# A fused attention and gated feed-forward kernel: another way in for the first quad's keys and queries, and a new order

## The chip, the cores and the metric

The kernel runs on one core of one Trainium2 chip. The metric is the device time of one execution in microseconds (us), the median of three runs.

The core has five engines that matter here: TensorE (PE, with PEld for its weight loads), VectorE (DVE), ScalarE (ACT), GpSimd (POOL) and SyncE (SP). Each engine takes its instructions in the order in which the program issues them, and waits on semaphores for what other engines and DMAs produce. DMAs are issued by POOL, SP and ACT, each into a queue of its own; all of them share 16 DMA engines. In this kernel only DMAs that POOL issues change the type of the data on the way (fp32 in DRAM, bf16 in SBUF).

## The reference

```python
# q, k, v: (8, 12, 448, 64) fp32; w_gate, w_val: (768, 1536); w_out: (1536, 768)
scores = (1 / sqrt(64)) * q @ k.T
attn   = max(scores, 0) ** 2 / 448
y      = attn @ v                              # (8, 12, 448, 64)
x      = y.transpose(0, 2, 1, 3).reshape(3584, 768)
out    = (max(x @ w_gate, 0) * (x @ w_val)) @ w_out
```

It is attention with a squared ReLU in the place of the softmax, then a feed-forward block with a ReLU gate. All inputs and the output are fp32.

## The kernel before, in words

**Tiling.** Four heads of one batch make a *quad*; there are 8 batches of 3 quads. A sequence of 448 is split into 7 blocks of 64. For each quad the keys lie in partitions 64 to 127 of a `raw` tile and the queries in partitions 0 to 63, in bf16. The `raw` tiles of the first two batches lie in `gvT`, a tile that is needed for other things only later (`early_raw`), so the trace names them `gvT`. Keys and queries must be transposed, so that the head dimension lies in partitions: the first six quads on PE against an identity matrix (L503 and L510 for batch 0, L550 for batch 1), with copies out of PSUM into `qkT` on DVE or ACT (L478, L476); the other 18 quads by a permuting copy on DVE into the one buffer `perm` (L574) and two DMA transposes that SP issues (L580).

**Attention.** A score step S is a group of four 64x64-tiled matmuls into two PSUM banks for each key block (L648), then a ReLU out of PSUM on ACT or DVE (L659, L661) and a square on ACT or DVE (L671, L673). Then come the products with the values, PV (L690), and a copy into `xT` (L706 on ACT, L708 on DVE). In batch 0 the queries are split: the first three blocks (192 columns, `QT` = 3) are loaded, transposed and used first, the other four later (`q_late`, transposed at L510).

**Feed-forward.** Batches 0 and 1 use plain products with `wg` and `wv` (L755, ReLU on ACT at L763, product on DVE at L765). The other batches use Strassen's scheme in pairs (L864), with sums of the weights made by DVE; the output products are L979, in the same scheme, and the results go out through SP's queue (L951).

**What sets the order.** Nothing is scheduled at run time: `plan` (L228) simulates the machine with a list of costs and emits the instructions in order of their planned start. PE's order is given by hand-over letters, `PE_ORDER`: a lower-case letter takes the next but so many of the list of attention operations, an upper-case letter the same of the feed-forward list. `LOAD_ORDER` does the same for POOL's list of loads. All other operations (`others`: copies, ReLUs, squares, stores, DMA transposes) are placed by the planner when they can start; `AHEAD` gives each a wait, in tenths of a microsecond around the letter m, that moves it against its rivals. `Res` holds, for each buffer, the planned time from which it is free; `Buf.pick` takes the buffer that is free first. In `commit`, a buffer's release is written down when its last reader is planned, from that reader's planned end; the planned end of a DMA can still move afterwards, as `flow` shares the DMA engines between loads and transposes. While PE would idle in the first 32 us, `plan` puts in matmuls on constants, which `filler` makes (L1133, on a tile that a memset at L1120 fills).

**The first loads.** `load_qk` (L429) makes for each quad a load of the keys, all seven blocks, and in batch 0 a load of the first three query blocks, all by `dma_in` on POOL (L388, the helper's line for all of them). With the letters before, POOL issues in this order: keys and queries of quad 0, keys and queries of quad 1, queries of quad 2, keys of quad 2, then late queries and values. `transpose_first` makes for quad 0 two PE operations: T0 for the first three blocks, of keys and queries together (12 transposes), and T0k for the other key blocks (16 transposes); T0k also waits for `key_ops`, which is empty before. `PE_ORDER` begins with T0, T0k and score steps of quad 0. The transposes of quads 1 and 2 (at L503 too) come further on. The identity matrix is made by DVE, until 3.15 us in the trace.

Of the kernel before, what the change touches and what calls it, by code (L numbers as in the profile page):

```python
# [8 lines left out]
FP32 = mybir.dt.float32  # L9
# [6 lines left out]
class Res:  # L16


    def __init__(self, n):
        self.free = {i: 0.0 for i in range(n)}  # L20


class Buf:
# [7 lines left out]
    def pick(self, now=0.0):  # L31

        best = None
        for i in self.among:
            if all(i + w in self.res.free for w in range(self.width)):
                t = max(self.res.free[i + w] for w in range(self.width))
                if best is None or max(t, now) < max(best[0], now):
                    best = (t, i)
        return best


class Op:


    def __init__(self, engs, emit, deps=(), alloc=(), reads=(), mode=None, grp=None):
        self.engs, self.emit = engs, emit
        self.deps, self.alloc, self.reads = list(deps), list(alloc), list(reads)
        self.mode, self.grp = mode, grp
        self.load = self.land = self.share = 0.0
        self.kind = self.behind = None  # L50
        self.xbar = 0
        self.start = self.end = self.eng = None
        for b in self.reads:
            b.readers += 1


class Planner:
# [5 lines left out]
    TO_LOAD, LOADED = 2.35, 0.95  # L63
    TO_TURN, TURNED, TURN = 1.7, 0.8, 3.65
    ISSUE = 0.28
    FILL_FROM = 0.4
    FILL_COLD = 5.5
    FILL_UNTIL = 32.0
# [13 lines left out]
    QT = 3  # L82
# [6 lines left out]

    def __init__(self, banks):  # L90
        self.banks = banks
        self.t = {"POOL": 1.25, "DVE": 0.85, "ACT": 2.0}
        self.ops = []
        self.mode = None
        self.dma_t = 0.0
        self.queues = [], []
        self.loads = []
# [21 lines left out]
    def best(self, op):  # L119
        r = self.ready(op)  # L120
        if r is None:
            return None
        c = None
        for e, (occ, busy) in op.engs.items():
            if e in ("DVE", "ACT"):
                r = max([r] + [d.end + self.MARGIN for d in op.deps if d.load])
            s = max(r, self.t.get(e, 0.0))
            if e == "PE" and op.mode != self.mode:
                s = max(r, self.t.get(e, 0.0) + self.SWITCH)
            f = s + busy + (self.BIAS if e == "DVE" and len(op.engs) > 1 else 0.0)  # L130
            if c is None or f < c[0]:
                c = (f, s, e)
        return c[1], c[2], r
# [27 lines left out]
    def commit(self, op, s, e):  # L161
        assert op.behind is None or op.behind.start is not None
        op.start, op.eng = s, e
        occ, busy = op.engs[e]
        now = self.now(op)
        self.t[e] = s + occ
        op.end = s + busy
        if e == "PE":
            self.mode = op.mode
        if op.load:  # L170
            self.loads.append(op)
            self.transfer(0, op, s + self.TO_LOAD, op.load)
        elif op.xbar:
            self.transfer(1, op, s + self.TO_TURN, self.TURN)
        else:
            op.end += op.land
        for b in op.alloc:
            t, b.idx = b.pick(now)
            assert t <= s + 1e-6
            for w in range(b.width):  # L180
                del b.res.free[b.idx + w]
            b.last = op.end
        for b in op.reads:
            b.readers -= 1
# [8 lines left out]
PE_ORDER = (  # L193
    'aaceccaacbcbacaeibbeccabaaecabAAacaFAccACaaabgcbaaNKJKATAHaaaJCICcebeJEEIbbFbaaGADFafabBABEabaBBAAabfeAKTLabKK'
    'CCGbaCDCAhecddHBBbbaDGACafbdaDDbaaFCAAbgbdAAacACBbaAAhcbbCaabABBbaDAAAebbaCcaaBIABCBcBABEEBAADCBAGAAHAEBBCBAAB'
    'DfaAADaaCABAcBBABaaACBAacbabDAAFCAACBCFCHBAEBCcBAAACbaAACAGAabbBABaaBCADAecbEACAaAFebaBACEAabEEFABfaFgaaABbdiA'
    'caCeaGBABBecdCAcbaAAAABfabaAEKADBAQAAEAAACBAAAbaDBAbbBDABAdaGCAAaabAAECAaBABBAAbaAIBAAbbaDAAbcAAJBCBAHAAFacBFA'
    'CbaACBACAAgbaAECEACBAedCAAbaaAFCAAAAAeaaaICcaAAbaAABAaaaaBBcbaCJEACaBEJAKAADBAACABAAABCBBBACBCDCBAABAAAADADHCB'
    'DCBICHABCFBHACAFEBEHBABCAEGBBDBBDCCECAAAGBABBABBBCGEAABBCBCCBABBABBBA'
)  # L200
# [4 lines left out]
AHEAD = (  # L205
    'mlmmmolklollknkknkmplknmkjnnnmolnlmmnqlkmoqokonmjkmkmokimmkloohjrnlghglokjjklmmqngmhtlhprneoficpkmjjsfnnpwrtpg'
    'arogqkpqrainsvngkgjgjzorsopgfnlrljmjoprmpskjjdbhgmmttnkmrlwpellhjpnjkqpqrlnlqlskbktfsijmkppnnjgkqllpmfhrkrlloh'
    'qtorjsllojjfkgpprlrhkmnppqlqoljlpmlnnrlooorlohholmjnlpofrwqmnfloogmisphjnnnhijlkqilojnokqkiomoorllqohglslmmmhn'
    'smlowookpgijmqkqmpjjrflkinkjiimhqpqommkljnnonompjslgpppjhornftieqplmirwlkthrihsurmosnrjfnmgvnhjnsrqoslhomntmol'
    'mvliqeknljmkmqsqlhmpsilnjklimmapnrqlnmdjgokqqnnorpigtjqitsoomkggjihpntqtqnenkpkiiuoposrepoqlnthjmkplplkkkkmsio'  # L210
    'irqvpnimlemgqspnnnbtukjkinnqjhgkkmqcisldokjnmqknkmklklofqnlpfnknqhlmknomgljilsiknjsnijlipknjmmpkjnrjlmqepmnflh'
    'ghknornoimjpoljkpmoqjiorpofnlplnnkrbmqpgompihkkkisqinkijffhlqpurmqpovfmgmgnnoorlompkoljpnnlqomlkopskhoihmkmnok'
    'onoiooemgipikpjimfknjomqmoipontjlkopgooljjlpmrjkifmhohpdjloliqokpmrligmhsufqrtosfrhrggpronqqkkmjmmlsqqlqtqoooq'
    'gmqikmklrspkmjrmonpihjponiinpmhmogphpmpnjqmklkoonlipgilmkmjnkjingpnqkmojsnklmkjrqmpmklhgknllfrlgqkjknmlfjnrrmp'
    'slmrmnnnikmonninkjmmmqjlikpqqmnjohpijopklkn'
)


# [74 lines left out]
def kernel(  # L293
# [10 lines left out]
    nc = tc.nc  # L304
# [3 lines left out]
    B, H, S, D = q.shape  # L308
# [5 lines left out]
    NT = S // P2  # L314
# [10 lines left out]
    QT = Planner.QT  # L325
# [29 lines left out]
    hT = pool.tile([128, KF, 2 * S], BF16, name="hT")  # L355
# [28 lines left out]
    others, pool_ops = [], []  # L384


    def dma_in(dst, src, n_desc, us, deps=(), alloc=(), share=0.25):
        op = Op({"POOL": (0.5 + 0.0004 * n_desc,) * 2}, lambda: nc.gpsimd.dma_start(out=dst(), in_=src),  # L388
                deps=deps, alloc=alloc)
        op.load, op.share = us, share  # L390
        pool_ops.append(op)
        return op
# [31 lines left out]
        o = 2 * NQ * 4 * NT * D + (NQ * b + g - 3) * n  # L424
        return flat[:, o:o + n].rearrange("p (h t d) -> p h t d", h=2, t=NT)

    FIRST_K = {(0, 0): 0.75, (0, 1): 2.4, (0, 2): 1.25}

    def load_qk(b, g):  # L429
        st = quads[(b, g)] = Quad()  # L430
        hs = slice(4 * g, 4 * g + 4)
        early = b < NEARLY
        st.raw_buf = None if early else Buf(r_raw)
        st.raw = lambda: early_raw(b, g) if early else raw_t[st.raw_buf.idx]
        src = lambda x, t0=0, t1=NT: x[b, hs].rearrange("h (p t) d -> p h t d", t=NT)[:, :, t0:t1]
        st.key_ops = []
        if (b, g) == (0, 0) and Planner.SPLIT:
            st.load_k = lambda t0, t1: dma_in(lambda: st.raw()[64:128, :, t0:t1], src(k, t0, t1), 256, 0.16 * (t1 - t0))
            k_op = st.load_k(0, QT)
        else:  # L440
            k_op = dma_in(lambda: st.raw()[64:128], src(k), 256, FIRST_K.get((b, g), 1.1),
                          alloc=[] if early else [st.raw_buf])
        if b == 0:
            st.load_q = lambda t0, t1: dma_in(lambda: st.raw()[0:64, :, t0:t1], src(q, t0, t1), 256, 0.17 * (t1 - t0))
            q_op = st.load_q(0, QT)
        else:
            q_op = dma_in(lambda: st.raw()[0:64], src(q), 256, 1.1)
            q_op.behind = None if early else k_op
        st.qk_ops = [k_op, q_op]
        if (b, g) == (0, 0) and Planner.SPLIT:  # L450
            st.key_ops = [st.load_k(QT, NT)]

    def load_v(b, g):
        st = quads[(b, g)]
# [669 lines left out]
    def filler(us, cold):  # L1124

        pb = bank([7, 6, 5, 4, 3, 2, 1, 0])
        total = int(us * (1200 if cold else 2400))
        n = (total + S - 1) // S
        width = max(64, total // n)

        def emit():
            for _ in range(n):
                nc.tensor.matmul(ps[:, pb.idx, :width], lhsT=still[:, :128], rhs=still[:, :width], start=True, stop=True)  # L1133

        return Op({"PE": (us, us)}, emit, deps=[still_op], alloc=[pb], reads=[pb])

    for g in range(NQ):
        load_qk(0, g)
# [106 lines left out]
```

## Time and profile before

| what | value |
|---|---|
| median of three runs | 404.07 us (403.68 to 406.75) |
| the profiled execution's own time | 403.12 us |
| its span in the trace | 401.3 us, granted TensorE clock 0.999 |
| PE busy | 391.8 us (98%), of it 8.4 us filler matmuls at L1133 |
| DVE busy | 323.7 us (81%) |
| ACT busy | 273.6 us (68%) |
| POOL busy | 75.6 us (19%), issuing DMAs |
| POOL's DMA queue | 23.60 MB written, 43.4% of 16 engines' span |
| SP's and ACT's queue | 18.89 MB |
| read from HBM | 47.19 MB |

The span is the stretch from the first to the last instruction that the profiler recorded; the execution's time has 1.8 us around it. A line of the timeline gives start, length, engine, line of the kernel, operation, output<-input, how many instructions are merged, and in brackets the idle time of the engine just before it and what ended that. A line of the table by stage gives the busy time of the engines in a stretch, with the number of instructions. PE counts as busy with filler matmuls too, so their time has to be taken off. All tiles of a kind have one name: `gvT` covers the early `raw` tiles, `ps` all PSUM banks.

### The profile page before, as it was taken

The page shows a single profiled execution, that of the slowest core. Times are in us where ns is not written, and L with a number is a line of the kernel's source. Part 1 is how long each engine was busy: PE and PEld are TensorE (multiplying, and loading weights), DVE is VectorE, ACT ScalarE, POOL GpSimd, SP SyncE. Part 2 cuts the span into 40 slices and gives each one's busy share as a digit, 9 for nine tenths or more (in the row PEclk, how much of TensorE's full clock was granted, in tenths as well). Part 3 has the DMA queues.
Part 4 walks back from the last instruction along what each step waited for, and adds up shares of the span by engine and source line. Part 5 has one row for each costly group of instructions (what it writes and reads, how often), then busy time and mean ns, then how long its engine had stood idle before and what let it go on. Part 6 is the DMA issues. An engine that isn't in the chain of part 4 may idle for free.

```text
span 401.3 us, 8739 instructions
## 1 busy us (share of the span) xinstructions
PE 391.8 (98%) x3471; PEld 208.7 (52%) x3471; DVE 323.7 (81%) x563; ACT 273.6 (68%) x402; POOL 75.6 (19%) x121
## 2 busy tenths in 40 slices
PE   8899999999999999999999999999999999999995
PEld 4576655454555554544445554444455555555563
DVE  4896777999899869989989978889878857758662
ACT  4897777788898547959878767778678854333221
POOL 8954541013212200213100121400100000000000
PEclk9999999999999999999999999999999999999999
DMA  8999999995996972386968697770503320000255
GB/s 116 191 200 200 199 183 191 175 113 77 166 127 138 195 140 36 41 115 80 111 113 147 145 160 107 101 118 9 73 23 80 80 59 2 0 0 2 59 125 133
DMA packets 77305, 43.44 MB, mean 108 GB/s; under 512 B 40912, under 2 KB 77264, under 8 KB 77264
## 3 DMA queue, kind: packets, MB, share of 16 engines
q0 software_dynamic: 34896, 23.60, 43.4%
q1 hardware_dynamic: 42048, 18.89, 26.0%
q8 instruction: 27, 0.44, 0.4%
q10 hardware_dynamic: 320, 0.39, 0.3%
q14 instruction: 14, 0.11, 0.1%
HBM read 47.19 MB, written 11.01 MB: 145 GB/s over the span
## 4 chain that ended last, share of the span: by engine, by line
PE 74%; DMA 16%; issue 6%; POOL 2%; DVE 1%; SPq 0%; DVEq 0%; POOLq 0%
PE ps L864 36%; PE ps L979 18%; PE ps L755 8%; PE ps L648 6%; PE ps L690 5%; DMA qkT<-perm 5%; DMA wg<-in_moe_w_gate_dram 5%; DMA vv<-in_v_dram 3%; DMA gvT<-in_v_dram 2%; DMA gvT<-in_k_dram 1%; POOL vv L388 1%; DVE perm L574 0%; POOL gvT L388 0%; POOL raw L388 0%; DVE at L661 0%
## 5 line engine op out<-in xcount | busy, mean ns | idle before, releaser
L659 ACT ACTIVATE at<-ps 128x896 bf16<-128x896 f32 (+3 forms) x119 | 105.5, 911 | 21.2 <-PE ps L648 20.6
L811 ACT COPY f<-ps 128x448 f32<-128x448 f32 x101 | 53.1, 533 | 46.8 <-PE ps L864 31.7
L671 ACT ACTIVATE at<-at 128x896 bf16<-128x896 bf16 (+2 forms) x72 | 66.8, 938 | 2.3 <-DVE at L661 1.2
L673 DVE TENSOR_TENSOR at<-at 128x896 bf16<-128x896 bf16 (+3 forms) x99 | 59.0, 612 | 5.5 <-ACT at L659 4.5
L661 DVE TENSOR_SCALAR at<-ps 128x896 bf16<-128x896 f32 (+4 forms) x52 | 54.5, 1050 | 6.3 <-PE ps L648 6.0
L388 POOL DMA_DIRECT2D vv<-in_v_dram x44 | 26.6, 610 | 136.3 <-PE ps L648 133.9
L648 PE MATMUL ps<-qkT 64*64 64x448 bf16 (+2 forms) x756 | 50.3, 338 | 2.0 <-ACT at L659 0.9
L864 PE MATMUL ps<-sx,wv 128*128 128x448 bf16 x216 | 50.8, 353 | 0.0
L864 PE MATMUL ps<-xT,gvT 128*128 128x448 bf16 x216 | 50.2, 353 | 0.0
L864 PE MATMUL ps<-xT,wg 128*128 128x448 bf16 x216 | 50.1, 353 | 0.0
L864 PEld LDWEIGHTS <-gvT 128*128 128x128 bf16 x324 | 31.0, 98 | 30.6 <-issue 2.7
L979 PEld LDWEIGHTS <-sh 128*128 128x128 bf16 x312 | 29.2, 98 | 23.9 <-issue 4.7
L979 PEld LDWEIGHTS <-hT 128*128 128x128 bf16 x270 | 25.6, 98 | 19.9 <-issue 3.4
L979 PE MATMUL ps<-wo,hT 128*128 128x384 bf16 x192 | 35.4, 326 | 0.0
L690 PE MATMUL ps<-at,vv 64*64 64x448 bf16 (+2 forms) x700 | 33.9, 328 | 0.2 <-DMA vv<-in_v_dram 0.2
L648 PEld LDWEIGHTS <-qkT 64*64 64x64 bf16 x756 | 18.9, 105 | 27.7 <-issue 23.8
L969 DVE SCALAR_TENSOR_TENSOR o<-ps,f 128x384 f32<-128x384 f32 x41 | 22.5, 554 | 12.6 <-PE ps L979 7.9
L813 ACT ACTIVATE f<-ps 128x384 f32<-128x384 f32 x38 | 18.6, 492 | 20.3 <-PE ps L979 20.0
L755 PE MATMUL ps<-xT,wv 128*128 128x448 bf16 (+2 forms) x180 | 31.0, 316 | 0.3 <-DVE hT L765 0.3
L864 PEld LDWEIGHTS <-wv 128*128 128x128 bf16 x216 | 20.3, 98 | 20.8 <-issue 3.0
L864 PEld LDWEIGHTS <-wg 128*128 128x128 bf16 x216 | 20.6, 98 | 20.1 <-issue 1.8
L755 PE MATMUL ps<-xT,wg 128*128 128x448 bf16 (+2 forms) x180 | 30.9, 315 | 0.1
(71 smaller groups left out, 488.8 us busy)
## 6 DMA issues: line engine op xcount, KB each, us to landing
out_dram<-o SPq DMA_DIRECT2D x108, 96.0 KB, 2.2
vv<-in_v_dram POOLq DMA_DIRECT2D x44, 112.0 KB, 5.3
raw<-in_k_dram POOLq DMA_DIRECT2D x18, 224.0 KB, 5.0
raw<-in_q_dram POOLq DMA_DIRECT2D x18, 224.0 KB, 7.5
wo<-in_moe_w_out_dram POOLq DMA_DIRECT2D x4, 576.0 KB, 15.4
wv<-in_moe_w_val_dram POOLq DMA_DIRECT2D x5, 384.0 KB, 11.3
wg<-in_moe_w_gate_dram POOLq DMA_DIRECT2D x5, 384.0 KB, 11.0
gvT<-in_k_dram POOLq DMA_DIRECT2D x6, 224.0 KB, 5.7
```

Source lines behind the costliest of these rows:

```text
L388: op = Op({"POOL": (0.5 + 0.0004 * n_desc,) * 2}, lambda: nc.gpsimd.dma_start(out=dst(), in_=src), deps=deps, alloc=alloc)
L648: nc.tensor.matmul(banks()[64 * j:64 * j + 64, z, h2], lhsT=self.k_of(j, h2, k), rhs=self.q_of(j, h2), start=True, stop=True)
L659: nc.scalar.activation(self.at_of(i, m), banks(), AF.Relu)
L661: nc.vector.tensor_scalar_max(self.at_of(i, m), banks(), 0.0)
L671: nc.scalar.activation(a, a, AF.Square)
L673: nc.vector.tensor_tensor(a, a, a, ALU.mult)
L690: nc.tensor.matmul(ps[64 * h2:64 * h2 + 64, ps2.idx + j, :n], lhsT=st.v_of(j, h2, c), rhs=self.at_of(c)[64 * j:64 * j + 64, 0, h2], start= ...
L755: nc.tensor.matmul(ps[:, pb.idx, z * n:(z + 1) * n], lhsT=w[:, kd, fc], rhs=xT_t[xbuf[b].idx][:, kd, cols], start=(kd == 0), stop=(kd == K ...
L811: nc.scalar.copy(dst, src)
L864: nc.tensor.matmul(ps[:, pb.idx, :S], lhsT=w(g)[:, fc], rhs=rhs, start=start and g == 0, stop=stop and g == KH - 1, skip_group_check=True)
L969: op = Op({"DVE": V384}, lambda: nc.vector.scalar_tensor_tensor(o_t[ob.idx], ps[:, pb.idx, :OH], float(out_scale), f_t[fb.idx][:, :OH], AL ...
L979: nc.tensor.matmul(ps[:, pb.idx, :OH], lhsT=lhs(kf), rhs=rhs(kf), start=start and kf == 0, stop=kf == FH - 1, skip_group_check=True)
```

## The change

There are four parts.

1. The keys and the first three query blocks of quad 0 no longer come by POOL's queue. Three fp32 loads put them into a corner of `hT` (not used yet at that time), seen as fp32: SP loads the first three key blocks, ACT the first three query blocks, SP then the other four key blocks. Two copies on DVE convert them to bf16 into the `raw` tile: one of 128 partitions for the first three blocks, one of 64 partitions for the other key blocks. T0 depends on the first, T0k on the second. The planner gets costs for these operations (`TO_HW`, `hw`), for ACT's table load, and for a slower PE in the first 6 us (`COLD`).
2. `FIRST_K`, the planner's transfer time of the first keys, has new values.
3. The planned release of a buffer that a DMA transpose reads (`perm`) is asked again each time (`Res.at`), from the transpose's planned end as it then stands.
4. `PE_ORDER`, `LOAD_ORDER` and `AHEAD` have new letters. `LOAD_ORDER` is two letters shorter (two loads fewer on POOL), `AHEAD` six longer (three loads, the table load and two conversions more).

```diff
 class Res:
+        self.by = {}
+
+    def at(self, i):
+        t, op = self.free[i], self.by.get(i)
+        return t if op is None else max(t, op.end + Planner.LATE[1])
...
 class Buf:
-                t = max(self.res.free[i + w] for w in range(self.width))
+                t = max(self.res.at(i + w) for w in range(self.width))
...
 class Planner:
+    TO_HW = 1.3
+    COLD = 6.0, 1.6
...
-        self.t = {"POOL": 1.25, "DVE": 0.85, "ACT": 2.0}
+        self.t = {"POOL": 1.25, "DVE": 0.85, "ACT": 0.74, "SP": 0.7}
...
-                r = max([r] + [d.end + self.MARGIN for d in op.deps if d.load])
+                r = max([r] + [d.end + self.MARGIN for d in op.deps if d.load and not d.hw])
...
+        if e == "PE" and s < self.COLD[0] and op.kind != "fill":
+            occ, busy = occ * self.COLD[1], busy * self.COLD[1]
...
-        if op.load:
+        if op.hw:
+            self.transfer(0, op, s + self.TO_HW, op.load)
+        elif op.load:
...
+                b.res.by.pop(b.idx + w, None)
...
+                    if op.xbar:
+                        b.res.by[b.idx + w] = op
...
 PE_ORDER = (
-    'aaceccaacbcbacaeibbeccabaaecabAAacaFAccACaaabgcbaaNKJKATAHaaaJCICcebeJEEIbbFbaaGADFafabBABEabaBBAAabfeAKTLabKK'
+    'aaccdabaabcialbabbbaebbbaacdfhafcBBADDaabbabgaZLBKMBAccabaHGCFFCFFdagbaJJlbdHHcbaAEFaabaEbaGBBAAAhgccaBAMTHJGC'
...
 LOAD_ORDER = (
-    'aaaabacebaacbacaaeccbaaidceokbdacgeeafafiaegeahcdgdfdcacabdddbddaalllacacccaaalaiccbddagaabddahdeacanlcahjbhca'
-    'bdaabba'
+    'aaaafcbaaaaicaaedcbbthddaaacchcefhbdiggagaaecddaggcaddaadbccddaabgeiibaanaafaabcaacchdgackiafacacaammkbddaeeca'
+    'aabba'
...
-    FIRST_K = {(0, 0): 0.75, (0, 1): 2.4, (0, 2): 1.25}
+    FIRST_K = {(0, 1): 1.1, (0, 2): 2.2}
+
+    def first_loads(st, src):
+        n = 4 * NT * D
+        wide = hT.rearrange("p k s -> p (k s)").bitcast(FP32)[:, :n].rearrange("p (h t d) -> p h t d", h=4, t=NT)
+
+        def load(eng, queue, x, rows, t0, t1, us):
+            op = Op({eng: (0.48, 0.5)}, lambda: queue.dma_start(out=wide[rows, :, t0:t1], in_=src(x, t0, t1)))
+            op.load, op.share, op.hw = us, 0.25, True
+            others.append(op)
+            return op
+
+        def convert(deps, rows, t0, t1, us):
+            op = Op({"DVE": us}, lambda: nc.vector.tensor_copy(st.raw()[rows, :, t0:t1], wide[rows, :, t0:t1]), deps=deps)
+            op.kind = "wide"
+            others.append(op)
+            return op
+
+        table = Op({"ACT": (1.3, 1.3)}, lambda: None)
+        k0 = load("SP", nc.sync, k, slice(64, 128), 0, QT, 0.5)
+        q0 = load("ACT", nc.scalar, q, slice(0, 64), 0, QT, 0.5)
+        k1 = load("SP", nc.sync, k, slice(64, 128), QT, NT, 0.65)
+        table.deps.append(q0)
+        others.append(table)
+        st.qk_ops = [convert([k0, q0], slice(0, 128), 0, QT, (0.46, 0.55))]
+        st.key_ops = [convert([k1], slice(64, 128), QT, NT, (0.6, 0.7))]
+        st.load_q = lambda t0, t1: dma_in(lambda: st.raw()[0:64, :, t0:t1], src(q, t0, t1), 256, 0.17 * (t1 - t0))
...
     def load_qk(b, g):
-        if (b, g) == (0, 0) and Planner.SPLIT:
-            st.load_k = lambda t0, t1: dma_in(lambda: st.raw()[64:128, :, t0:t1], src(k, t0, t1), 256, 0.16 * (t1 - t0))
-            k_op = st.load_k(0, QT)
+        if (b, g) == (0, 0):
+            first_loads(st, src)
+            return
...
+        op.kind = "fill"
```

Read through the lists, the new letters begin as follows. PE: T0, T0k, three score steps of quad 0, the transposes of quad 1, the fourth score step of quad 0, the transposes of quad 2, then score steps of quads 1 and 2. POOL: keys and queries of quad 1, keys and queries of quad 2, first values of quad 1, late queries. The first feed-forward product is the 34th PE operation, where it was the 31st.

More of the change, by code (lines that the diff above doesn't have):

```diff
@@ L50, in __init__ @@
         self.kind = self.behind = None
+        self.hw = False
         self.xbar = 0
@@ L188, in commit @@
                     b.res.free[b.idx + w] = b.last
+                    if op.xbar:
+                        b.res.by[b.idx + w] = op
         self.ops.append(op)
 PE_ORDER = (
-    'aaceccaacbcbacaeibbeccabaaecabAAacaFAccACaaabgcbaaNKJKATAHaaaJCICcebeJEEIbbFbaaGADFafabBABEabaBBAAabfeAKTLabKK'
[L195 to L198, printed above, removed]
+    'aaccdabaabcialbabbbaebbbaacdfhafcBBADDaabbabgaZLBKMBAccabaHGCFFCFFdagbaJJlbdHHcbaAEFaabaEbaGBBAAAhgccaBAMTHJGC'
+    'HCCabaCECAffccbBHcaaEFEDAgddcccDaaCADBfgAbbdaBDCAbaAAhccbCCbaDaBAAadBeAabdaBJbaDBACBDGcBFAAFADABHAAAHABDBCBAAB'
+    'DfaAADaaCABAcBBABaaABBAacbabDAGDAEABBCAIEAEACABAAcACbaAACAGAabbBABaaBCADAecbEACAaAFebaBACEAabEEFAfaBFgaCAabdAC'
+    'bbaGBAdeCBecdCAaaaAAAABaebaAEKADBAQCBADADABAAAbaDBAbbBDCDAAdaFBAaabBACDaABBCCBBBAbaBADEbbaEBEDBIABAdIAGbdABAEC'
+    'FaaDAHEBBBABABBacBDBAebeaAAaaaABDAAAAeaaaICcaABaaAABAaaeaBBcaaABIDCaBEJABJADCAKACHABEBBABBACBCDCBAABAAAADADHCB'
     'DCBICHABCFBHACAFEBEHBABCAEGBBDBBDCCECAAAGBABBABBBCGEAABBCBCCBABBABBBA'
@@ L201 @@
 LOAD_ORDER = (
-    'aaaabacebaacbacaaeccbaaidceokbdacgeeafafiaegeahcdgdfdcacabdddbddaalllacacccaaalaiccbddagaabddahdeacanlcahjbhca'
-    'bdaabba'
+    'aaaafcbaaaaicaaedcbbthddaaacchcefhbdiggagaaecddaggcaddaadbccddaabgeiibaanaafaabcaacchdgackiafacacaammkbddaeeca'
+    'aabba'
 )
 AHEAD = (
-    'mlmmmolklollknkknkmplknmkjnnnmolnlmmnqlkmoqokonmjkmkmokimmkloohjrnlghglokjjklmmqngmhtlhprneoficpkmjjsfnnpwrtpg'
-    'arogqkpqrainsvngkgjgjzorsopgfnlrljmjoprmpskjjdbhgmmttnkmrlwpellhjpnjkqpqrlnlqlskbktfsijmkppnnjgkqllpmfhrkrlloh'
@@ L208 @@
[L208 to L212, printed above, removed]
@@ L213 @@
-    'onoiooemgipikpjimfknjomqmoipontjlkopgooljjlpmrjkifmhohpdjloliqokpmrligmhsufqrtosfrhrggpronqqkkmjmmlsqqlqtqoooq'
-    'gmqikmklrspkmjrmonpihjponiinpmhmogphpmpnjqmklkoonlipgilmkmjnkjingpnqkmojsnklmkjrqmpmklhgknllfrlgqkjknmlfjnrrmp'
-    'slmrmnnnikmonninkjmmmqjlikpqqmnjohpijopklkn'
+    'llklmmnlolormnnqmomolmmhjmlmnnniplpololmjqoqmkllqqmomnhllolkigknlliqpkqgqhhhpqogripspsnhsinomjqncpmldpsiolpgos'
+    'nxnssahoxepjkxshnmpurdqleptrhouljadnftprjqbropuvhflfhdfknnnlopjlqneqemimhfflntuammtntnkmndqigsmjlfdakntnsugjnw'
@@ new lines @@
+    'iprmrfstopfuolmjkcjgrnrjrknoqzjsoqlkiknlllnrlnpqqlnfjokniolpnfsyqlpdjomglirqjjpnpkiiiloilpjpqosmionomrknpneelr'
+    'mmnjgoqnjowllqpdggknkrcsnjxalifoinmlgmrpqmemekpqggrofqkoljnvodnukniznbsqwgelvijqhqcnxrqqpupqhfmlduikmnosrjumfn'
+    'mrjnlgmspioniwljfgotxxlhkmpajpnsithsfjnqmojmggaljpspporhgeyitsnurndkhdojopmqktcpcmkknkeupkzqihuqrmooikspqvqejn'
+    'lpqvfkinnqrjhqrdldqjpnnqaxshkqfphomgjhhkmfkqsaehtqlokuilkojfmcpmolfmjmqgnlmllsdkjilulhnjtnhijhnknjknokjlrjlmqe'
+    'pmnelheginormmgmlpolkkpnorjjpromfkmolnmksamprimmqglkjnisqgohmjdgempkuqnmtmvdpglaonqolhnmmnokepmrhmoljgmqolemal'
@@ L216 @@
+    'ligqmomkmnrkgeclmgemkilfanaootqnglphpomosjilunblfnopaogiponnwahqpflsofqmsofngattjvtuvwfngmggsommpqhjnigoourpms'
+    'wrskopcpsllnlhwtslnlqoplmndgppjlhmmnlonilhrjplnlnilhntojhoffmlimhnnkdpkmtripklvnmloikopqrlmmkejplletlfsljmmmkg'
+    'jnpskptlornlpojkoppmhmiilmoqijikpoolnlofnglnpmjmn'
 )
@@ L449, in load_qk @@
         st.qk_ops = [k_op, q_op]
-        if (b, g) == (0, 0) and Planner.SPLIT:
-            st.key_ops = [st.load_k(QT, NT)]
     def load_v(b, g):
@@ L1133, in emit @@
                 nc.tensor.matmul(ps[:, pb.idx, :width], lhsT=still[:, :128], rhs=still[:, :width], start=True, stop=True)
-        return Op({"PE": (us, us)}, emit, deps=[still_op], alloc=[pb], reads=[pb])
+        op = Op({"PE": (us, us)}, emit, deps=[still_op], alloc=[pb], reads=[pb])
+        op.kind = "fill"
+        return op
     for g in range(NQ):
```

## The prediction

> **What bounds the kernel now.** I first read the table of busy time by stage, all engines, for the first 60 us.
>
> ```profile
> 5.55:12.00 6.45, 5.95 (x137) 3.78 (x137) 3.96 (x9) 4.59 (x8) 5.53 (x10) 1.00 1.32 181
> 12.00:22.00 10.00, 8.65 (x251) 6.12 (x253) 9.77 (x17) 9.46 (x16) 8.61 (x13) 1.00 1.54 191
> 22.00:35.00 13.00, 12.00 (x239) 9.14 (x231) 10.62 (x19) 11.90 (x18) 5.35 (x8) 1.00 1.36 200
> 35.00:60.00 25.00, 24.87 (x271) 15.68 (x269) 18.06 (x30) 18.72 (x29) 13.36 (x19) 1.00 1.40 194
> ```
>
> Columns: stage, length, then PE, PEld, DVE, ACT, POOL busy, clock, DMA share, GB/s. From 35 us PE is busy 99% of the time; in other stages of the same table 100 to 300 us is 99.7%. What can be won lies before 35 us. From 12 to 22 us DVE is busy 98% and ACT 95%: that stage is bound by the ReLU and square work, not by PE. From 5.55 to 12 us DVE idles 2.5 us and ACT 1.9 us: they wait for data.
>
> The same table for the filler line (L1133, matmuls on constants) says how much of PE's busy time is no work.
>
> ```profile
> 0.00:5.55 5.55, 4.11 (x13) 1.65 (x13) 1.00 0.57 67
> 5.55:60.00 54.45, 4.33 (x20) 1.46 (x20) 1.00 1.41 194
> ```
>
> PE idles 54.45 - 51.47 = 2.98 us from 5.55 to 60 us and fills 4.33 us; with the 5.55 us before the first real matmul that is 12.9 us without useful work. This is all a better start can take from. The timeline shows what it waits for.
>
> ```profile
> 0.73 1.28 ACT L476 ACT_TABLE_LOAD   x1 [0.73 <-PEq L1229]
> 1.24 0.75 POOL L388 DMA_DIRECT2D gvT<-in_k_dram  x1 [0.80 <-POOLq L1229]
> 1.98 0.63 POOL L388 DMA_DIRECT2D gvT<-in_q_dram  x1
> 2.58 0.64 POOL L388 DMA_DIRECT2D gvT<-in_k_dram  x1
> 3.19 1.27 POOL L388 DMA_DIRECT2D gvT<-in_q_dram  x2
> 4.39 0.68 POOL L388 DMA_DIRECT2D gvT<-in_k_dram  x1
> 5.58 0.90 PE L503 MATMUL ps<-ident,gvT 128*64 128x128 bf16 x28
> 6.51 0.40 PE L648 MATMUL ps<-qkT 64*64 64x192 bf16 x8
> 8.28 1.13 PE L503 MATMUL ps<-ident,gvT 128*64 128x128 bf16 x28 [0.44 <-DMA gvT<-in_q_dram]
> 10.18 1.03 PE L503 MATMUL ps<-ident,gvT 128*64 128x128 bf16 x22
> ```
>
> The first quad's keys are issued at 1.24 and its queries at 1.98 by POOL; the transposes (28 in 0.90 us, 32 ns each) start 3.6 us after the second issue. The second quad's transposes start at 8.28, after a wait for queries; the third's at 10.18. These three starts are what the change can move.
>
> **Part 1, first quad by SP and ACT.** ACT's first instruction starts at 0.73 and SP is released at 0.7, so both loads are issued at about 0.73. The trace has no fp32 load. Nearest rows: the output stores of the same two queues, 96 KB, land in 2.2 us (least 2.1); the quickest POOL load of this tile 3.5, the median of the 96 KB ones 4.9. I take the stores, as the queue is the same, and add for size: keys and queries (three of seven blocks each) are 384 KB of fp32; the stage writes 200 GB/s of bf16, so reads 400 GB/s (over the span the POOL queue wrote 23.60 MB, and 47.19 MB were read); 384 - 96 KB more is 0.7 us. Landing: 0.73 + 2.2 + 0.7 = 3.6 (2.8 to 5.6). The other four key blocks, 256 KB behind them, 0.65 later: 4.3.
>
> The conversion, 128x768 f32 from SBUF to bf16, is in no row either. Below: the permute copy, bf16 from SBUF, 128x1792 in 0.626 us, so 768 in 0.27 by proportion. Above: the casts of f32 out of PSUM (L708), 128x384 in 0.56 and 128x896 in 1.07, so 0.94 for 768 and 1.20 for the 1024 of the second conversion. The cast is the nearer row, since the type is the same. DVE is free (idle 3.15 to 6.15): first conversion 3.6 to 4.55, the 12 transposes on PE from 4.6; second 4.55 to 5.75, the other 16 transposes 5.8 to 6.3, and the first score matmuls, behind both in PE's order, at about 6.4 against 6.51. So the first quad gains 0.1 us; at the low price (0.27 and 0.36) it gains 1.1; if the loads take as POOL's do, it loses 1. I take 0.1. The two conversions cost 2.1 us of DVE, hidden by its idle 3.0 us here; the same work in the 98% stage would cost its whole length.
>
> [...] The permute copy took 0.95 us at 45.47 while POOL issued DMAs at 45.16 and 45.99, and 0.62 or 0.63 in the later rows that I read.
>
> ```profile
> 45.16 0.84 POOL L388 DMA_DIRECT2D wv<-in_moe_w_val_dram  x1 [1.38 <-DMA wv<-in_moe_w_val_dram]
> 45.47 0.95 DVE L574 COPY perm<-raw 128x1792 bf16<-128x1792 bf16 x1
> 45.99 0.60 POOL L388 DMA_DIRECT2D vv<-in_v_dram  x1
> ```
>
> So a copy beside POOL's issues cost 0.33 us more, and POOL issues without a break from 1.24 to 7.5 us. [...]
>
> **Part 2, POOL's list.** Two issues (0.75 and 0.63) leave POOL's head, so the second quad's keys go out at 1.24 instead of 2.58, 1.34 earlier, its queries likewise. Decoded, the letters give second keys, second queries, third keys, third queries. The bytes ahead of the second queries are the same as before, and they begin to flow about 1 us earlier (writes appear at 2.6 us now; the new queues' by 2). The second transposes' data are then there at 8.28 - 1.3 = 7.0, and PE, from 6.4 with three score groups ahead of them, arrives at 7.0: **1.2 us gained**. Third quad: keys issued 1.8 earlier, queries 0.6 earlier, total bytes through both the same: also about 1.2 earlier (0.6 to 1.8). From here ACT and DVE are full and carry a shift on; the loads behind, at 200 GB/s until 60 us, lie as much earlier (0.6 MB of fp32 moved before 3.6 us, 1.6 us of the stream at most). With 35 us reached 1.2 us earlier, PE, 99% busy from there, ends 1.2 earlier.
>
> **Part 3, permute buffer.** The recount only changes where the planner puts the permute copies. DVE stood 3.0 us in 3 waits for the one buffer (the view of waits, DVE perm L574 on DMA qkT<-perm). Behind them PE lost little: 0.3 at 64.26 (behind hT) and 0.3 (L979 behind f, L817). Bounds 0 to 0.6; I take 0.3.
>
> **Part 4, the order searched anew.** Decoding the letters against the lists of operations gives 139 changes of tile shape in PE's planned order before and 139 after. A change costs about 0.12 us (8 score matmuls 0.50 alone in the chain, 2x0.19 by the 0.189 of one 448-column matmul). So PE's work stays: 0, with ends -0.8 (all waits after 60 us) and +2 (a new wait). The sum: 1.2 + 0.3 = **1.5 us**. The profiled execution took 403.12 us (span 401.3, 1.8 around it): 401.6. The median shown is 404.07, 0.95 above; with the same difference, **402.6 us**.
>
> **Rivals.** *Nothing gained* (16%): the conversions wait for POOL's issues, 0.6 us each, or ACT's table load (1.28 us) goes ahead of the query load and the first conversion starts at 4.9. Either way the second conversion ends at 7, the first scores start at 7.6, the second quad's transposes, in order behind them, at 8.2, and at most 0.4 us is left: 403.7 to 404.1. For it: the 0.95 row; POOL has no break. Against: both fit into DVE's idle time at least in part.
> [...]
>
> *Late transposes, slower* (18%): batch 2's scores need the DMA transposes behind the one permute buffer (first row from the chain that ended last, the others from the timeline).
>
> ```profile
> 47.92 13.35 DMA qkT<-perm
> 61.39 0.63 DVE L574 COPY perm<-raw 128x1792 bf16<-128x1792 bf16 x1 [1.59 <-DMA qkT<-perm]
> 65.49 0.38 PE L648 MATMUL ps<-qkT 64*64 64x448 bf16 x4
> ```
>
> The first lands at 61.3 and is needed at 65.5: 4.2 us spare. In the new order its first scores have 1.3 us less matmul time before them (49.6 against 51.0, from the listed costs), and with the shift of 1.5 are due at 62.7; its queries have 384 KB more ahead of them (1.9 us at 200 GB/s), less the shift: landing 61.7. One us is spare. A landing more than 1.0 us later stops PE, and one more than 2.5 later makes the kernel slower than before. Loads this late took up to 20.2 us to land at most (median 6.2), so 4 us is possible: 402.6 + 3 = 405.6; two such stalls, 408.5. For: the thin margin. Against: 99.7% busy PE in the stages that were ordered in the same way.
>
> *More gained* (10%): the fill and idle time of 5.55 to 35 us (7.2 us) is cut by half as well: 402.6 - 3 = 399.6.
>
> **Chances.** Forecast (gain of 0.5 to 2.8) 56%, the rivals 16, 18 and 10%. A measurement tells about 1% (4 us) from no change. Below 400.0 is half of the last rival: 0.05. Above 408.1 is the worse part of the late transposes: 0.07. Within 1%: 0.88. The range from 400.6 to 405.4 leaves out some 6% below and 12% above; it takes in the first quad's ends (-1 to +1.1) and the order's.
>
> **What would show it.** ACT's and SP's loads at 0.7 to 1.3, ahead of the table load; two f32 to bf16 copies on DVE of 0.5 to 1.2 us each; transposes (L503 now) at about 4.6, second quad 7.0, third 9.0; filler from 5.55 on below 4 us; no wait of PE for qkT above 1 us between 58 and 75 us; permute waits on DVE below 3 us. A first quad later than 6.5, a PE wait in 58 to 75 us, or equal starts with a PE share below 99% after 60 us would make it wrong.

## The result, and the profile after

The changed kernel takes 405.63 us (median of 22 runs, 404.80 to 406.11); the kernel before took 403.32 us in 22 runs beside them (402.23 to 406.75). The ratio is 1.0051, with a 95% interval of 1.0038 to 1.0063: **slower by about 2.1 us**, where 1.5 us less was forecast, and just above the range. The profiled execution took 405.24 us, with a span of 403.5.

The table by stage of the changed kernel (stage, length, busy time of PE, PEld, DVE, ACT, POOL, clock, DMA share, GB/s):

```profile
5.55:12.00 6.45, 4.87 (x83) 2.93 (x85) 3.20 (x6) 2.30 (x4) 5.16 (x10) 1.00 1.35 200
12.00:22.00 10.00, 9.56 (x211) 5.84 (x205) 7.45 (x17) 6.09 (x11) 7.69 (x10) 1.00 1.51 193
22.00:35.00 13.00, 12.87 (x284) 9.60 (x283) 11.89 (x20) 12.22 (x19) 6.76 (x10) 1.00 1.41 200
35.00:60.00 25.00, 24.96 (x300) 16.38 (x296) 19.72 (x31) 20.07 (x31) 9.95 (x14) 1.00 1.34 197
```

From 5.55 to 12 us PE is busy 1.1 us less than before, ACT half as long. From 12 to 22 us DVE and ACT are no longer full (7.45 and 6.09 of 10 us, where it was 9.77 and 9.46): they wait for PE. From 35 to 300 us PE idles 0.04 us where it idled 0.95: there the new order is better. From 22 to 35 us idle time fell too, from 1.0 to 0.1 us, but filler takes 3.0 us there and took 0.4 before, so that stretch is not better. The filler line (L1175 now), by stage:

```profile
6.11:12.00 5.89, 1.08 (x3) 0.28 (x3) 1.00 1.37 196
12.00:22.00 10.00, 3.47 (x11) 1.08 (x11) 1.00 1.51 193
22.00:35.00 13.00, 3.01 (x14) 1.20 (x14) 1.00 1.41 200
```

Filler after the first transposes has grown from 4.3 to 7.6 us. The timeline of the changed kernel, the first 18 us; L452 are the fp32 loads, L458 the conversions, L545 the transposes of batch 0, L690 the score matmuls, L1175 the fillers:

```profile
0.73 0.73 ACTq L452 DMA_DIRECT2D hT<-in_q_dram  x1
0.74 1.65 SPq L452 DMA_DIRECT2D hT<-in_k_dram  x2
1.39 3.53 PE L1175 MATMUL ps<-woT 128*128 128x446 bf16 x9 [1.39 <-DVE woT L1162]
5.27 0.79 DVE L458 CAST gvT<-hT 128x768 bf16<-128x768 f32 x1 [2.12 <-DMA hT<-in_k_dram]
6.11 0.85 PE L545 MATMUL ps<-ident,gvT 128*64 128x128 bf16 x12 [1.19 <-DVE gvT L458]
7.24 0.69 DVE L458 CAST gvT<-hT 64x1024 bf16<-64x1024 f32 x1 [1.19 <-DMA hT<-in_k_dram]
7.99 0.58 PE L545 MATMUL ps<-ident,gvT 64*64 64x64 bf16 x14 [1.03 <-DVE gvT L458]
8.38 0.37 PE L690 MATMUL ps<-qkT 64*64 64x192 bf16 x2
10.51 1.54 PE L545 MATMUL ps<-ident,gvT 128*64 128x128 bf16 x22
13.05 1.53 PE L545 MATMUL ps<-ident,gvT 128*64 128x128 bf16 x22
15.32 2.17 PE L1175 MATMUL ps<-woT 128*128 128x398 bf16 x6
```

Two things stand here. The fp32 loads are late: the list of DMA issues has them landing 3.5 (queries), 4.4 (first keys) and 5.7 us (other keys) after the issue, so the second conversion starts at 7.24 and the first scores come at 8.38 (before: 6.51). And PE is slow: six fillers of 398 columns take 2.17 us, their weight loads 0.33 us apart, which is about half of the rate at 22.9 us (eight of 444 columns in 1.67 us). Before, the weight loads of the fillers stand 0.36 us apart until 4.59 us and some 0.18 from there on: full rate.

```profile
4.23 0.15 PEld L1133 LDWEIGHTS <-woT 128*128 128x128 bf16 x1 [0.21 <-issue]
4.59 0.48 PEld L1133 LDWEIGHTS <-woT 128*128 128x128 bf16 x3 [0.21 <-issue]
```

In the changed kernel the first group of fillers ends at 4.92 us, as planned for loads landing by then; PE idles 1.2 us, works 0.85, idles again 1.0, and runs at half rate until about 17 us. The stage table's clock says 1.00 throughout, so it does not show this: the trace's record of the granted clock begins only when full rate is granted, at 17.5 us (before: at 4.6), and what lies ahead of the record is counted as full. The mean granted clock over the span was 0.987 in 14 of the 22 runs and 0.999 or 1.0 in the other 8, with much the same times.

### The profile page after: what moved, and what is told of

It reads as the page before. It is cut to its first block, busy times and chain, and to the rows that moved or that the text cites. A ratio compares the mean times of both kernels' runs of the same rounds, so it can differ in the third digit from the quotient of the medians.

```text
span 403.5 us, 8740 instructions
## 1 busy us (share of the span) xinstructions
PE 395.2 (98%) x3475; PEld 210.6 (52%) x3475; DVE 325.5 (81%) x564; ACT 274.9 (68%) x403; POOL 74.4 (18%) x119
## 4 chain that ended last, share of the span: by engine, by line
PE 90%; DMA 8%; POOL 1%; issue 0%; DVE 0%; POOLq 0%
PE ps L906 36%; PE ps L1021 25%; PE ps L797 13%; PE ps L690 9%; PE ps L732 7%; DMA wg<-in_moe_w_gate_dram 4%; DMA gvT<-in_k_dram 3%; POOL gvT L404 0%; PE ps L592 0%; POOL vv L404 0%; DVE o L1011 0%; POOLq L1273 0%
## 5 line engine op out<-in xcount | busy, mean ns | idle before, releaser
L701 ACT ACTIVATE at<-ps 128x896 bf16<-128x896 f32 (+4 forms) x120 | 106.4, 906 | 24.4 <-PE ps L690 23.7
L853 ACT COPY f<-ps 128x448 f32<-128x448 f32 x103 | 54.1, 532 | 45.7 <-PE ps L906 30.2
L715 DVE TENSOR_TENSOR at<-at 128x896 bf16<-128x896 bf16 (+4 forms) x103 | 61.5, 609 | 10.4 <-ACT at L701 9.3
L713 ACT ACTIVATE at<-at 128x896 bf16<-128x896 bf16 (+1 forms) x68 | 63.4, 947 | 2.1 <-DVE at L703 1.4
L690 PE MATMUL ps<-qkT 64*64 64x448 bf16 (+2 forms) x756 | 52.0, 345 | 0.4 <-ACT at L701 0.3
L906 PE MATMUL ps<-xT,gvT 128*128 128x448 bf16 x216 | 51.2, 353 | 0.0
L690 PEld LDWEIGHTS <-qkT 64*64 64x64 bf16 x756 | 19.9, 107 | 27.5 <-issue 22.4
L404 POOL DMA_DIRECT2D raw<-in_k_dram x18 | 11.3, 627 | 107.1 <-DVE perm L616 70.2
## 6 DMA issues: line engine op xcount, KB each, us to landing
wv<-in_moe_w_val_dram POOLq DMA_DIRECT2D x5, 384.0 KB, 10.5
```

Of the source, the lines that this page charges most:

```text
L690: nc.tensor.matmul(banks()[64 * j:64 * j + 64, z, h2], lhsT=self.k_of(j, h2, k), rhs=self.q_of(j, h2), start=True, stop=True)
L701: nc.scalar.activation(self.at_of(i, m), banks(), AF.Relu)
L713: nc.scalar.activation(a, a, AF.Square)
L715: nc.vector.tensor_tensor(a, a, a, ALU.mult)
L853: nc.scalar.copy(dst, src)
L906: nc.tensor.matmul(ps[:, pb.idx, :S], lhsT=w(g)[:, fc], rhs=rhs, start=start and g == 0, stop=stop and g == KH - 1, skip_group_check=True)
```

## The experiments

Theory A: the half rate costs the time. B: the late loads cost it by themselves. C: the new letters do. All ratios are to the kernel before on the same chip, with 95% intervals.

**More filler ahead of the first transposes.**

```diff
+    fills = []
     def filler(us, cold):
         ...
+        n += 6 if cold and not fills else 0
+        fills.append(n)
```

> The changed kernel with six more filler matmuls (446 columns) in the first group of fillers, ahead of the first transposes; nothing else. In the changed kernel that group ends at 4.92 us and PE then idles 1.19 us for the first conversion; weight loads of the fillers stand 0.33 us apart for 398 columns until 16.6 us, which is half the rate of those at 22.9 (8 of 444 columns in 1.67 us). Theory A, the half rate costs the time: the longer group reaches 6.0 us, full rate is there from about 4.7, the second and third quads' transposes take 1.1 instead of 1.9 us each, and the kernel wins 1.5 to 3 us on the changed one (403 to 404 us). Theory B, only the late fp32 loads cost it: PE runs faster but waits as long, less than 0.5 us is won. Theory C, the new letters cost it: the same as B here.

Measured: 402.43 us in the median of 12, in two groups: eight times from 401.78 to 402.67, with a mean granted clock of 0.998 to 1.0, and four from 405.63 to 406.40 with 0.987 to 0.991 (ratio of all 0.9988, 0.9959 to 1.0018). The profiled execution was of the second group, 406.40 us, and there the clock shows in the stage table:

```profile
5.55:12.00 6.45, 4.71 (x70) 2.31 (x68) 2.90 (x6) 1.57 (x3) 4.40 (x8) 0.83 1.31 188
12.00:22.00 10.00, 9.86 (x187) 6.19 (x187) 6.33 (x15) 6.41 (x10) 8.68 (x12) 0.60 1.48 187
```

The trace's record of the clock has full rate from 6.38 to 9.79 us and half rate from 9.79 to 20.03. So the longer group of fillers did bring full rate here, and it was lost again after the gap ahead of the second transposes:

```profile
9.03 0.44 PE L545 MATMUL ps<-ident,gvT 64*64 64x64 bf16 x16 [1.74 <-DVE gvT L458]
```

Same program, same chip, 3.8 us between the groups' medians, and clock and time go together. This is what A expects; the letters (C) are the same in both groups. In this execution the other keys landed 6.7 us after their issue, 1 us later than in the changed kernel, so which runs lose the rate may hang on the landing; 1 us of landing alone (B) does not make 3.8.

**The loads with the old letters; the new letters with the old loads; the recount alone.** In the first, `PE_ORDER`, `LOAD_ORDER` and `AHEAD` of before stand beside the new loads:

```diff
-        return t if op is None else max(t, op.end + Planner.LATE[1])
+        return t
```

> The three fp32 loads and two conversions as in the changed kernel, but with the letters of before (without the two for POOL's first loads, and m for the six new operations) and without the recounted release. Theory B (loads land at 5.1 and 7.2 us wherever the order comes from) and A: first transposes at about 6.1, the second sixteen at about 8.0, 1 to 3 us slower than before. Theory C: as fast as before or up to 1.5 us faster.

Measured: 429.44 us, ratio 1.0642 (1.0605 to 1.0679). In the second, POOL loads the first quad:

```diff
-        if (b, g) == (0, 0):
-            first_loads(st, src)
-            return
-    FIRST_K = {(0, 1): 1.1, (0, 2): 2.2}
+    FIRST_K = {(0, 0): 0.75, (0, 1): 2.4, (0, 2): 1.25}
```

> The letters of after and the recounted release, but the first quad loaded by POOL as before (two letters more for POOL, six fewer for the others, the planner's start values of before). Theory C (the new order costs the time): 1.5 to 3 us slower than before. Theories A and B: within 0.7 us of before, or faster.

Measured: 410.33 us, ratio 1.0153 (1.0124 to 1.0182). The third is the kernel before with `Res.at` and nothing else:

```diff
-                t = max(self.res.free[i + w] for w in range(self.width))
+                t = max(self.res.at(i + w) for w in range(self.width))
```

> The kernel before with the recounted release of the permute buffer alone, letters of before. By the prediction's third part 0.3 us is won (0 to 0.6), DVE's waits for the permute buffer fall from 3.0 us, and PE's two waits of 0.3 us at 64 and 204 us go. The rival: the letters were fitted to the old release, so moving the copies without them costs 0.3 to 1 us.

Measured: 414.68 us, ratio 1.0269 (1.0241 to 1.0297).

All three expectations missed by far: 26, 6 and 11 us, where 1 to 3 at most were expected. The stage table of the loads with the old letters shows where:

```profile
100.00:200.00 100.00, 94.05 (x740) 47.50 (x738) 81.68 (x138) 71.21 (x100) 15.81 (x26) 1.00 0.64 102
200.00:300.00 100.00, 93.52 (x762) 46.03 (x760) 81.69 (x143) 71.03 (x101) 16.44 (x27) 0.98 0.70 107
```

PE idles 12 us between 100 and 300 us, far from the first loads, where it idles 0.6 in the kernel before. The letters fit only the plan that they were searched for: a changed cost or release moves other operations, and the same letters then mean another order. So the three tell nothing on which of loads, letters and recount is the good or the bad part; they are only to be had together, and the other experiments change what is emitted without touching the plan.

**No gap on PE.** The six fillers, and seven more between the first quad's two groups of transposes:

```diff
+            def emit_late():
+                for _ in range(7):
+                    nc.tensor.matmul(ps[:, ps2k.idx, :S], lhsT=still[:, :128], rhs=still[:, :S], start=True, stop=True)
+                emit_slots(ps2k, range(QT, NT), n0)
-            opk = pe(lambda: emit_slots(ps2k, range(QT, NT), n0), 0.5, ...
+            opk = pe(emit_late, 0.5, ...
```

> The changed kernel with six more filler matmuls ahead of the first transposes and seven of 448 columns between the first twelve transposes and the other sixteen, so that PE has no gap from 1.4 us until the second conversion. In the run with the six alone 8 of 12 times were 401.8 to 402.7 us (clock 0.998 to 1.0) and 4 were 405.6 to 406.4 (0.987 to 0.991). [...] Rival, the two groups of times come from when the loads land: they stay two, in like shares.

Measured: 402.77 us (401.71 to 403.67, one group of nine, clock 0.998 to 1.0; under A times of 401.8 to 403.0 were expected, and two lie above), ratio 0.9952 (0.9927 to 0.9978). **This is faster than both kernels.** Its timeline:

```profile
8.09 0.44 PE L545 MATMUL ps<-ident,gvT 64*64 64x64 bf16 x16 [0.32 <-DVE gvT L458]
9.70 1.04 PE L545 MATMUL ps<-ident,gvT 128*64 128x128 bf16 x22
12.74 1.18 PE L1184 MATMUL ps<-woT 128*128 128x398 bf16 x6
29.55 1.77 PE L737 MATMUL ps<-at,vv 64*64 64x256 bf16 x56
```

The second transposes come at 8.09, no earlier than in the changed kernel (7.99), but the six fillers take 1.18 us instead of 2.17 and the second quad's 22 transposes 1.04 instead of 1.54. With the loads equally late, the rate alone is worth 1.0051 - 0.9952 = 0.0099 of the time, 4.0 us; in the two profiled executions the last matmuls start at 398.29 and 394.99 us, 3.3 us apart. The late loads by themselves (B) and the letters (C) are the same in both kernels, and with them this one is faster than before: neither makes the loss without the half rate.

**The kernel before with less filler.**

```diff
+        n -= 5 if cold and not fills else 0
```

> The kernel before with five of the thirteen first filler matmuls left out; loads and letters of before. PE's first busy stretch then ends near 4.3 us and it waits to 5.55 for the queries as before. Theory A: full rate is reached late as in the changed kernel, 2.5 to 4 us slower than before (406 to 408 us) in most runs, though no load came later. Rival, the rate matters only together with late loads: within 0.7 us of before.

Measured: 405.80 us (403.40 to 408.09 in 12 runs), ratio 1.0037 (1.0009 to 1.0064). The profiled execution, 408.05 us, has it as A says:

```profile
1.39 3.05 PE L1137 MATMUL ps<-woT 128*128 128x430 bf16 x8 [1.39 <-DVE woT L1120]
5.54 1.31 PE L503 MATMUL ps<-ident,gvT 128*64 128x128 bf16 x24 [1.10 <-DMA gvT<-in_q_dram]
10.54 1.64 PE L1137 MATMUL ps<-woT 128*128 128x438 bf16 x4
18.07 0.69 PE L1137 MATMUL ps<-woT 128*128 128x407 bf16 x3
```

0.41 us per filler at 10.5 us, 0.23 at 18; the record of the clock begins with full rate at 17.1 us. A gap ahead of the first transposes makes the old loads and letters slower as well, though by 1.5 us in the median and not 2.5 to 4; the runs form no two groups here.

**Three more fillers instead of six** (`n += 3`).

> The changed kernel with three more filler matmuls in the first group instead of six: PE is busy on end from 1.4 to about 6.0 us less a gap near zero to one of 0.2, then the transposes. [...]

Measured: 405.36 us in the median; two of 12 times at 402.2, the others from 404.37 to 407.26; ratio 1.0015 (0.9987 to 1.0043). Under A fast times were expected in a part of the runs, no more than the 8 of 12 with six, and the others at 405 to 406: there are two, but four lie between the groups (404.4 to 405.3), so there are not just two groups. The profiled execution was one of the two at 402.2: full rate from 7.14 us on (the first 12 transposes, at 5.96, take 0.85 us, the 16 at 8.09 take 0.44, as in the kernel without a gap), kept over a gap of 1.27 us ahead of the second transposes.

**POOL's first load later.** A memset on POOL ahead of its first load, one or three of them:

```diff
+    late = xT_t[0].rearrange('p k s -> p (k s)')
+    nc.gpsimd.memset(late[:, :2048], 0.0)
     for op in plan(first, att, ffn, others, pool_ops, still_op, filler, r_ps):
```

> The changed kernel with a memset on POOL (2048 columns of a tile not yet in use) ahead of its first load, so that the three fp32 loads have the DMA engines to themselves; its own time doesn't matter. Contention theory (the loads are late because POOL's share the 16 engines with them): keys land at 3.6 to 4.0 instead of 5.1, the other keys at 4.3 to 5.0 instead of 7.2. Rival (256 pieces of 768 or 1024 bytes on these queues take that long by themselves): 5.1 and 6.5 to 7.2 again.

> The changed kernel with three memsets on POOL ahead of its first load, 5.4 us by the 1.80 of the one in the run before, so that no load of POOL moves before about 8 us. With one memset the bulk of the keys had moved by 5.2 us but the landings stayed 4.5 and 5.8 us after the issue, a few late packets beside POOL's stream. Contention theory: the other keys now land at 5.2 to 5.6 us instead of 7.3, the first keys at 4.7 or earlier. Rival (pieces and receipt on these queues take it by themselves): 5.1 to 5.3 and 7.0 to 7.4 as in both runs before.

Measured: with one memset (first load of POOL at 2.48 instead of 1.24 us) the landings were 4.5, 3.5 and 5.8 us after the issue, as without; with three (6.21) 4.6, 3.7 and 4.7. So the other keys lose about 1 us to POOL's stream, and the rest of the lateness is the loads' own. (405.80 and 406.67 us, one run each.) The second run shows one thing more, in its timelines of POOL and DVE:

```profile
0.74 5.53 POOL L1259 MEMSET xT<- 128x2048 bf16 x3 [0.29 <-POOLq L1276]
5.46 1.22 DVE L458 CAST gvT<-hT 128x768 bf16<-128x768 f32 x1 [2.31 <-DMA hT<-in_k_dram]
```

The conversion that takes 0.56 us in the kernel without a gap takes 1.22 here: it ends 0.4 us after the memset.

**The other keys by ACT's queue**, with three fillers between the transposes:

```diff
-        k1 = load("SP", nc.sync, k, slice(64, 128), QT, NT, 0.65)
+        k1 = load("SP", nc.scalar, k, slice(64, 128), QT, NT, 0.65)
```

> The kernel without a gap on PE (six more fillers, and three before the second transposes instead of seven), with the other four key blocks issued by ACT right behind the queries instead of by SP behind the first keys. ACT's queue began to move at 2.1 us, SP's at 2.9, and SP's second load at 5.0. If ACT's queue lets it move from 3.9 us on, it lands at about 5.5 to 6, and the first scores come at about 7.2 instead of 8.5. Theory D, an earlier first quad is worth its full shift: 0.8 to 1.3 us faster than the kernel without a gap (402.8), so 401.5 to 402.0. Theory E, the start is hidden behind ACT's, DVE's and the loads' work until 35 us: within 0.4 us of 402.8, though the scores come earlier. Rival on the queue: the two queues share what makes their pieces, the load lands at 7 again, nothing moves.

Measured: 11 runs of 401.46 to 402.47 us, ratio 0.9945 (0.9917 to 0.9972), not to be told from 0.9952. The one profiled execution took 1025 us, so PE's times can't be read from it; in it the load landed 6.1 us after the issue, no earlier than on SP's queue (5.7). The first scores probably did not move, and D and E are not told apart.

**All of POOL's loads 1.24 us later at full rate**: the kernel without a gap, with one memset.

> The kernel without a gap on PE with one memset ahead of POOL's first load, so that all of POOL's loads are issued 1.24 us later. Theory F, the stream of loads sets when PE is full: 0.8 to 1.3 us slower than without the memset (403.6 to 404.1). Theory E' (ACT's and DVE's work on the first quads sets it): within 0.4 us of 402.8.

Measured: 402.40 us, ratio 0.9953 (0.9926 to 0.9980), the same as without the memset. The intervals are about 1.1 us to each side, as wide as the loss that F expects; the traces tell more. PE's second transposes start at 9.95 us (9.70 without the memset) and a group of scores at 17.95 (17.70): 0.25 us behind at both points, not 0.8 to 1.3. The start of POOL's stream has about 1.2 us to spare; F falls.

**No wait for the first quad.**

```diff
-            op = Op({"DVE": us}, lambda: nc.vector.tensor_copy(st.raw()[rows, :, t0:t1], wide[rows, :, t0:t1]), deps=deps)
+            op = Op({"DVE": us}, lambda: nc.vector.memset(st.raw()[rows, :, t0:t1], 0.125), deps=deps)
```

> Part of the computation is left out: the two conversions are memsets of the same tiles that wait for no load (the fp32 loads are still issued), so the first quad's keys and first queries are a constant; two more fillers in the first group instead of six, none between the transposes. The first quad's transposes can start when the fillers end, at about 5.2 us, and its first scores come at about 6.3 instead of 8.5 in the kernel without a gap; all else waits as there. Theory D, the late first quad costs time even at full rate: 1 to 2.2 us faster than the kernel without a gap (ratio 0.9952 to the kernel before), so a ratio of 0.990 to 0.993. Theory E, the first quad's start is hidden: ratio 0.994 to 0.997. If the full rate comes late here too in some runs, those are 3 us longer and are read apart.

Measured: 400.16 us (399.83 to 400.42), ratio 0.9916 (0.9886 to 0.9946). Its timeline:

```profile
8.24 1.03 PE L545 MATMUL ps<-ident,gvT 128*64 128x128 bf16 x22
28.06 1.77 PE L732 MATMUL ps<-at,vv 64*64 64x256 bf16 x56
```

PE's second transposes lie 1.46 us earlier than in the kernel without a gap (8.24 for 9.70), the products with the values at 28 us 1.49 (28.06 for 29.55), and the last matmul starts 1.51 us earlier (393.48 for 394.99). The ratio is 0.0036, 1.45 us, less; the two intervals overlap, so the shift in the traces is the better evidence. D holds: PE's fixed order passes the first quad's lateness on in full, while the loads behind it have slack.

## Why the prediction was wrong, point by point

**What bounds the kernel**: the reading that only the first 35 us can be won stands for both kernels, but not for their neighbours: PE is full from 35 us on only with letters that fit the plan, and loses 12 us there without.

**Part 1, the loads**, is the first step that failed, and it is a term mis-sized. Landings were put at 3.6 and 4.3 us from the 96 KB stores plus their size; they measured 5.1 and 7.2. The rows that I set aside, POOL's 3.5 and 4.9 us, were nearer to the 3.5, 4.4 and 5.7 us from issue to landing; I took the same queue's row although its direction and the number of pieces differ. The other keys came 2.1 us behind the first, not 0.65; about 1 us of that goes with POOL's stream. I took "loses 1" as the worst end, and the first scores lost 1.9 us on the kernel before. The conversions were sized too high (0.94 and 1.20 against 0.79 and 0.69), which could not help. The first scores came at 8.38 instead of 6.4, 2.0 us late, and PE hands such a delay on one to one (without the wait, 1.46 us earlier at the start were 1.51 us at the last matmul).

**The step that was missing** turned the sign. I had the fillers' spacing of 0.36 and 0.18 us in the trace of before, and the change itself gives the planner a slower PE until 6 us (`COLD`); I put PE's rate at nothing in the sum. A filler is not free time: its group is emitted for a planned gap and does not stretch when a load is late. In the changed kernel it stops at 4.92, the transposes wait to 6.11 and again to 7.99, and the full rate comes at 17.5 us instead of 4.6: 4.0 us by the ratios.

The records of the clock show what a gap does. In the profiled runs with six more fillers, with one memset and with three, full rate came at 6.38, 4.39 and 5.37 us. It was taken back after 3.41 us, of which PE had worked 1.7, 0.9 and 1.8, and half rate then lasted 10.24 us, though PE worked 8.3 to 10.2 us of these. In the run with three more fillers PE worked 2.5 us of the first 3.41 and kept the rate. A mean clock of 0.987, as in the first three of these executions and in 14 runs of the changed kernel, is what 10.24 us at half rate make of 403.5 us. What sets the 10.24 us stays open.

How long PE worked on end before its first gap goes with how many times were near 402 us: 3.5 us in the changed kernel, none of 22 runs; about 5.9 with six more fillers, 8 of 12; no gap, 9 of 9. Work on end is not all of it: in the changed kernel PE works without a break from 7.99 to 17.0 us, and full rate comes only at 17.5. What decides when full rate is granted was not shown.

**The copy beside POOL's issues**, weighed in part 1 by the row of 0.95 us: it shows here too, and is small. The first conversion took 0.79 us in the changed kernel, beside three POOL issues of 1.91 us together; in the run with six more fillers it took 0.56 and the three issues beside it 2.14. In both executions the one or the other is 0.23 us longer. In the runs with three more fillers and without a gap the conversion took 0.56 as well; beside a long memset it took 1.22. The rival built on that row (nothing gained) was not what happened.

**Part 2, POOL's list**: the second and third quad's transposes came at 10.51 and 13.05, not 7.0 and 9.0; at full rate at 9.70 and 11.28. The 1.2 us did not exist in this form: PE stands behind the first quad's second transposes in its fixed order, whatever has landed for the others, and POOL's loads can start 1.24 us later at no cost that shows.

**Part 3, the permute buffer**: DVE's 3.0 us of waits for it are gone in the changed kernel, as said, and so are the waits of 0.3 us on PE at 64 and 204 us; idle time on PE from 35 to 300 us fell from 0.95 to 0.04 us, more than the 0.3 forecast. How much of this is the recount and how much the letters is not settled, as neither works without the other.

**Part 4, the order**: equal counts of changes of tile shape were taken for equal cost, with ends -0.8 and +2. The kernel without a gap is 1.9 us faster than before, with its quads 1.1 to 1.4 us later; what is left to make it so is the order together with the recount, though no run has them alone. In the profiled executions PE's busy time less the fillers is 382.1 us there and 383.4 before, and idle and filler time together come to 18.1 and 18.0 (one execution each, and the ends of matmuls are modelled). So the gain seems to lie in PE's own work, the term put at 0; counts could not show that. The late transposes of the second rival did not occur: no wait of PE for qkT is in the list of waits.

**The number** 402.6 us is close to the 402.3 of the first experiment's faster group, but that is luck, for it comes by other terms: first quad 2.0 late instead of 0.1 early, order and recount better than 0.3. The rival to have named is the one that happened: the filler ends before the data come, and PE works at half rate for some thirteen more microseconds.

## What to carry to other kernels

Where a kernel warms PE with fillers, size them from the latest landing that the trace allows and not from the planned one; here two gaps, of 1.19 and 1.03 us, cost 4.0 us by the ratios. Too many fillers delay the real work: in the profiled run with six more the first transposes started at 6.76 us, though their data were converted at 5.75. For a load of a kind that the trace doesn't have, take the slowest near row for the path and the fastest only as an end. An order searched for a plan belongs to that plan's costs: parts of such a change can't be tested by undoing one in the source, only by changing what is emitted.

## What the runs showed that was not expected

- Plain fp32 loads of 192 and 256 KB on SP's and ACT's queues, in pieces of 768 and 1024 bytes, landed 3.4 to 4.6 and 4.7 to 6.7 us after the issue, over all the runs here; in the changed kernel their issues took 0.73 to 0.83 us each, and the packets of ACT's load moved from 2.2 us on, those of SP's first from 2.8, of SP's second from 4.8.
- Moving the permute buffer's release by itself, a change to the planner alone, cost 10.9 us (2.7%).
- The mean granted clock of 0.999 or 1.0 does not prove full rate: 8 of the 22 runs of the changed kernel read so, the profiled one among them, whose rows show half rate until 17 us and whose record of the clock begins at 17.5.
- Late in the kernel the rate is lost for a shorter time: in the runs of the recount alone and of the loads with the old letters, both with a granted clock of 0.98 in the stage from 200 to 300 us, PE worked 1.6 and 1.1 us of a stretch of 3.41 us that ended near 223 us, and half rate followed for 3.41 us, not 10.24.
